# A Strassen stage turned into a graph with one fixed order per engine, and two more weight sets multiplied by seven products in the second layer

## The chip, the core and the metric

The kernel runs on one core of a Trainium2 chip. The metric is the device time of one execution in microseconds; before the change the median of three runs is 882.67 us (882.40 to 883.54). The engines are TensorE (PE in the profile; PEld are its weight loads), VectorE (DVE), ScalarE (ACT), GpSimd (POOL) and SyncE (SP), whose queue issues the DMAs here.

## What is computed

Causal attention with a decay for 4 x 8 heads of 576 tokens and 64 columns, and on its output, 2304 tokens of 512 columns, a mixture of four experts that all see every token:

```python
x = attention(q, k, v, f)                       # 2304 x 512
p = probs / (probs.sum(-1, keepdims=True) + 1e-09)
out = np.zeros((2304, 512))
for e in range(4):
    h = np.maximum(x @ w1[e], 0.0)              # 512 -> 1024
    out += p[:, e:e + 1] * (h @ w2[e])          # 1024 -> 512
```

The 4 x 1024 hidden columns are cut into 16 pairs p of 2 x 128 columns; a pair holds the rows of w1 and w2 that belong to them.

## The kernel before, in words

Every matmul of the expert layers is made of three in float16 (high x high, high x low, low x high halves), which keeps float32 accuracy. Attention and the experts of the first five chunks of 256 tokens come first and fill TensorE until about 566 us. The last four chunks (5 to 8, 1024 tokens) are done by the Strassen stage behind it, and the change is in this stage alone.

**First layer of a pair** (`Big`, L1339 on). The 512 columns of x and the 256 hidden columns of the pair are blocks of a 2 x 2 Strassen-Winograd product with seven products instead of eight. A product (`product`, L1346) is six matmuls of 128x512 into a PSUM bank. Seven steps `l1(s)` per pair follow each product by copies to SBUF (ScalarE, L1381), sums with what is there (VectorE, `plus`, L1386), relu (ScalarE, L1390) and the splitting into a high and a low half of h (`halves`: ScalarE L1369, VectorE L1370). For pairs whose second layer is also done by seven products, four more sums s 1 to s 4 of blocks of h are made on GpSimd (`sum`, L1395), each with its own halves.

**Second layer of a set** (`Second`, L1457 on). The sets are (0), (1), (2, 3), (4, 5) up to (14, 15). A set in `PLAIN` = (0, 1, 6, 7, 12, 13) takes 16 parts, each six matmuls of 128x512 for two pairs; every second one is followed by a gather of 128x512 into the accumulator (`gather`, VectorE, L1129). Any other set takes seven products: 28 parts of six matmuls of 128x256, each followed by a gather of 128x256. A bank is reused by the next product on it only after that gather has read it. Parts are dealt out between the first-layer steps of the pairs two places ahead, in a queue that is spread evenly (`give`); the set (14, 15) ends the kernel alone.

**Weights.** `split_1(p)` loads the float32 block of w1 (`raw_half`, L1237, 512 KB) and its ready float16 halves, makes four sums of blocks (GpSimd, L1232, tile wt), scales them (ScalarE, L1259), and splits them (ScalarE L1263, GpSimd L1264, tile bs). `split_2(p)` does the same for w2 where the set is not plain (tiles wu, bt; ScalarE L1304, VectorE L1308); for a plain pair it only loads the halves (tile bv).

**What sets the order.** TensorE's matmuls of the stage are chained one by one in program order (`in_line`). The other engines' instructions are placed by the framework's scheduler, which simulates a timeline, with a few hand-written bounds: weight steps come after the latest copy and gather (`in_turn`), the weight sums after the latest GpSimd sum (`pool`). The weight work of a pair is staged by hand over three places of the first-layer steps (`staged`).

Of the kernel before, what the change touches and what calls it, by code (L numbers as in the profile page):

```python
# [13 lines left out]
ALU = mybir.AluOpType  # L14
# [32 lines left out]
AHEAD_W = 6  # L47
JOBS = ((0, 0), (1, 0), (2, 0), (3, 0), (0, 1), (1, 1), (2, 1), (3, 1))
# [32 lines left out]
EXPONENT = 0x7F800000  # L81


@with_exitstack
def fused(ctx: ExitStack, tc: tile.TileContext, qk, v, f, probs, w, out):
# [907 lines left out]
    def w_pair(n):  # L993
        t = w_p.tile([128, 2, 1024], F16, tag="w", name=f"w{n}")
        wh[n], wl[n] = t[:, 0], t[:, 1]
        return t
# [117 lines left out]
    def gather(c, tt, sc, ps, times, d0=0, d1=DM):  # L1114
# [8 lines left out]
        if begun == {False}:  # L1123
            nc.vector.tensor_scalar(
                out=acc[c][:, tt, d0:d1], in0=ps, scalar1=sc, scalar2=None, op0=ALU.mult
            )
        else:
            gone.append(
                nc.vector.scalar_tensor_tensor(  # L1129
                    out=acc[c][:, tt, d0:d1],  # L1130
                    in0=ps,
                    scalar=sc,
                    in1=acc[c][:, tt, d0:d1],
                    op0=ALU.mult,
                    op1=ALU.add,
                )
            )
        done = [d for (_, _, d) in keys if seen[c, tt, d] == times[d // 256]]
        if done:
            a, z = done[0], done[-1] + 256  # L1140
            for o, r0, n in rows_of(c, tt):
                nc.sync.dma_start(out=out[r0 : r0 + n, a:z], in_=acc[c][o : o + n, tt, a:z])

# [43 lines left out]
    PLAIN = (0, 1, 6, 7, 12, 13)  # L1187
# [16 lines left out]
    def x_piece(i, k, op=None, *of):  # L1204
# [10 lines left out]
        if op is None:  # L1215
            x = x_of(k)
        else:
            x = xs_[k, i] = late.x.tile([128, 2, CH], F32, tag="wx", name=f"rx{k}_{i}", bufs=2)
            pool.append(nc.gpsimd.tensor_tensor(out=x, in0=x_of(of[0]), in1=x_of(of[1]), op=op))
# [3 lines left out]
    def sums(name, r, table):  # L1223
        part = lambda b: r[:, b[0], 256 * b[1] : 256 * b[1] + 256]
        if not hasattr(late, "x"):
            t = acc_p.tile([128, 4, 256], F32, tag="acc", name=name)
        else:
            t = late.x.tile([128, 4, 256], F32, tag="wt", name=name, bufs=2)
        w_of = lambda b: part(b) if type(b) is tuple else t[:, b - 1, :]
        for k, a, z, op in table:  # L1230
            with tc.issue_after(pool[-1].ins) if pool else nullcontext():
                nc.gpsimd.tensor_tensor(out=t[:, k - 1, :], in0=w_of(a), in1=w_of(z), op=op)  # L1232
        return t.rearrange("p k n -> p (k n)")

    def raw_half(p, k):
        r = wr_p.tile([128, 2, 512], F32, tag="wr", name=f"wr{NS + p}_{k}", bufs=4)
        nc.sync.dma_start(  # L1237
            out=r,
            in_=w[2 * p : 2 * p + 2, :, 512 * k : 512 * k + 512].rearrange("n p c -> p n c"),
        )  # L1240
        return r

    def split_1(p):
        if p >= 16:
            return ()
        r = raw_half(p, 0)
        t, u = (
            w_p.tile([128, 2, 1024], F16, tag="w", name=f"b{k}{p}") for k in ("w", "s")
        )
        one = t.rearrange("p n (s f) -> p n s f", s=2)  # L1250
        for n in range(2):
            nc.sync.dma_start(out=one[:, n], in_=wd[2 * p + n][:, :, :512])
        bw[p] = one, u.rearrange("p s (k f) -> p s k f", k=4)
        f = sums(f"wt{p}", r, SUMS)
        hi, lo = u[:, 0], u[:, 1]

        def scale(a):
            x = f[:, a : a + 512]
            nc.scalar.activation(out=x, in_=x, func=AF.Copy, scale=wsc[:, p // 2, 0:1])  # L1259

        def part(a):
            x, h = f[:, a : a + 512], hi[:, a : a + 512]
            nc.scalar.activation(out=h, in_=x, func=AF.Copy)  # L1263
            nc.gpsimd.tensor_tensor(out=lo[:, a : a + 512], in0=x, in1=h, op=ALU.subtract)  # L1264

        return (
            lambda: scale(0),
            lambda: (part(0), scale(512)),
            lambda: part(512),
        )  # L1270

    seconds = []

    def second_tile(name):
        i = len(seconds) % 8
        if i < 4:
            t = wr_p.tile([128, 2, 1024], F16, tag="wk", name=name, bufs=4)
        elif i < 6:
            t = w_p.tile([128, 2, 1024], F16, tag="w", name=name)
        else:  # L1280
            t = late.x.tile([128, 2, 1024], F16, tag="wx", name=name, bufs=2)
        seconds.append(t)
        return t

    def split_2(p):
        if p >= 16:
            return ()
        t = second_tile(f"bv{p}")
        one = t.rearrange("p n (s f) -> p n s f", s=2)
        for n in range(2):  # L1290
            nc.sync.dma_start(out=one[:, n], in_=wd[2 * p + n][:, :, 512:])
        if p in PLAIN:
            bv[p] = one, None
            return ()
        r = raw_half(p, 1)
        u = second_tile(f"bt{p}")
        bv[p] = one, u.rearrange("p s (k f) -> p s k f", k=4)
        f = sums(f"wu{p}", r, TSUMS)
        hi, lo = u[:, 0], u[:, 1]
        sc = wsc[:, p // 2, 1:2]  # L1300

        def upper(a):
            z = a + 512
            nc.scalar.activation(out=hi[:, a:z], in_=f[:, a:z], func=AF.Copy, scale=sc)  # L1304

        def lower(a):
            z = a + 512
            nc.vector.scalar_tensor_tensor(  # L1308
                out=lo[:, a:z],
                in0=f[:, a:z],  # L1310
                scalar=sc,
                in1=hi[:, a:z],
# [4 lines left out]
        return (  # L1317
            lambda: upper(0),
            lambda: (lower(0), upper(512)),
            lambda: lower(512),  # L1320
        )
# [7 lines left out]
    line, mark, pool, gone = [], [], [], []  # L1329
# [9 lines left out]
    class Big:  # L1339


        def __init__(self, p):
            self.p = p
            self.h, self.ps = {}, {}

        def product(self, m, bank, start):  # L1346
            if start:
                self.ps[bank] = ps_a.tile([128, 512], F32, tag="a", name=f"m{self.p}_{m}")
            ps = self.ps[bank]
            w_, b = PRODUCTS[m]  # L1350
            a, z = part_of(bw[self.p], w_)
            for k in range(2):
                o = slice(128 * k, 128 * k + 128)
                for i, (lhsT, rhs) in enumerate(((a, rh[b]), (a, rl[b]), (z, rh[b]))):
                    in_line(
                        out=ps,
                        lhsT=lhsT[:, o],
                        rhs=rhs[:, k, :],
                        start=(start and k == 0 and i == 0),
                        stop=(k == 1 and i == 2),  # L1360
                        skip_group_check=True,
                    )
            return ps

        def halves(self, b, x, op=ALU.mult, tag=None):

            t = late.h.tile([128, 2, 512], F16, tag=f"h{tag or b}", name=f"h{self.p}_{b}")
# [466 lines left out]
```

## Time and profile before

| | |
|---|---|
| median of three runs | 882.67 us (882.40 to 883.54) |
| profiled execution, its own time | 883.93 us |
| its span, first to last instruction | 882.1 us |
| TensorE busy | 864.4 us, 98% |
| VectorE busy | 643.0 us, 73% |
| ScalarE busy | 480.6 us, 54% |
| GpSimd busy | 372.6 us, 42% |

Busy time is the union of an engine's instructions, and neighbours overlap a little, so a mean duration is somewhat more than an instruction's place in its queue. An idle time is put down to what ended it (the releaser). The engine shares are means over stages; for this change the busy table of single stretches says more.

### The profile page before, as it was taken

Reading aid. Unit: us, or ns where it says so; the run is one execution under the profiler, and the core shown is the slowest. Engines: PE = TensorE matmul, PEld = TensorE weight load, DVE = VectorE, ACT = ScalarE, POOL = GpSimd, SP = SyncE. Lnnn points to the kernel's source line nnn. Section 1 sums busy time; section 2 is a strip of 40 time slices with the busy share of each in tenths; the row PEclk is TensorE's granted clock in tenths of the full one; section 3 lists DMA queues with packets and bytes.
Section 4 is the critical chain, followed back from the end, with each engine's and each line's share of the span. In section 5 each row is a group of like instructions: output and inputs, shape, how many; then the busy total and the mean of one; then the engine's idle time right before and its main releaser. Section 6 shows DMA issues by size and latency. Waiting matters only on the chain.

```text
span 882.1 us, 16028 instructions
## 1 busy us (share of the span) xinstructions
PE 864.4 (98%) x5699; PEld 556.8 (63%) x5699; DVE 643.0 (73%) x1390; ACT 480.6 (54%) x999; POOL 372.6 (42%) x421
## 2 busy tenths in 40 slices
PE   9999999999999999999999999999989999999998
PEld 5766666666766766667666766544456654666547
DVE  5766799868777888767678856456788657886586
ACT  5473645746565866555577644356555355554350
POOL 4253423542322432243232203827787437884160
PEclk9999999999999999999999999999999999999999
DMA  9989697799999999958979951533124332240003
GB/s 276 391 212 361 135 298 232 194 327 247 250 249 246 271 280 251 265 137 217 295 196 282 258 89 42 189 122 120 48 81 135 121 120 71 72 145 25 25 1 96
DMA packets 166589, 162.49 MB, mean 184 GB/s; under 512 B 104854, under 2 KB 129484, under 8 KB 166508
## 3 DMA queue, kind: packets, MB, share of 16 engines
q1 hardware_dynamic: 166508, 161.46, 65.9%
q8 instruction: 45, 0.74, 0.4%
q14 instruction: 36, 0.29, 0.1%
HBM read 115.65 MB, written 21.64 MB: 156 GB/s over the span
## 4 chain that ended last, share of the span: by engine, by line
PE 65%; POOL 10%; DVE 9%; DMA 6%; ACT 5%; issue 4%; SPq 1%; POOLq 0%; DVEq 0%; ACTq 0%
PE l L1100 18%; PE l L1057 16%; PE y L1335 8%; PE m L1335 8%; PE s L666 4%; POOL s L1395 4%; PE o L870 4%; PE l L1045 3%; POOL wt L1232 3%; PE s L689 2%; DMA raw<-in_qk 2%; POOL wu L1232 2%; DMA pt<-z 1%; DVE acc L1129 1%; ACT wt L1259 1%
## 5 line engine op out<-in xcount | busy, mean ns | idle before, releaser
L1057 PE MATMUL l<-y,w 128*128 128x256 f16 x1728 | 211.5, 273 | 0.0
L1057 PEld LDWEIGHTS <-w 128*128 128x128 f16 x1728 | 163.9, 98 | 40.1 <-issue 7.4
L1100 PE MATMUL l<-w,gh 128*128 128x512 f16 (+1 forms) x600 | 184.4, 392 | 2.8 <-DVE acc L1129 2.8
L600 POOL CAST q<-raw 64x320 fp32r<-64x320 f32 (+1 forms) x56 | 25.2, 452 | 224.9 <-PE s L689 101.5
L1100 PE MATMUL l<-w,gl 128*128 128x512 f16 x284 | 107.2, 379 | 0.3 <-DVE gl L1074 0.3
L716 ACT ACTIVATE p<-p,nm 128x384 f32<-128x384 f32 (+3 forms) x96 | 62.0, 646 | 64.6 <-DVE nm L701 64.5
L1129 DVE SCALAR_TENSOR_TENSOR acc<-y,scg,acc 128x256 f32<-128x256 f32 (+1 forms) x164 | 81.2, 515 | 14.9 <-PE y L1335 14.7
L1335 PE MATMUL m<-rh,bs 128*128 128x512 f16 x256 | 86.4, 379 | 0.0
L1100 PEld LDWEIGHTS <-gh 128*128 128x128 f16 x568 | 51.1, 98 | 51.9 <-issue 10.9
L607 POOL TENSOR_TENSOR kl<-raw,hi 64x576 fp32r<-64x576 f32 (+1 forms) x56 | 66.5, 1187 | 38.3 <-ACT hi L598 36.8
L701 DVE CUSTOM_DVE_ANT_0 p<-s,mask 128x384 f32<-128x384 f32 (+3 forms) x96 | 54.3, 572 | 28.2 <-PE s L666 25.4
L804 DVE SCALAR_TENSOR_TENSOR z<-p,rs,z 128x512 f16<-128x512 f32 x96 | 61.0, 677 | 18.9 <-ACT z L803 18.9
L1264 POOL TENSOR_TENSOR bs<-wt,bs 128x512 f16<-128x512 f32 x32 | 37.9, 1190 | 78.8 <-ACT bs L1263 77.8
L1074 DVE SCALAR_TENSOR_TENSOR gl<-l,gh 128x512 f16<-128x512 f32 x72 | 49.1, 682 | 24.0 <-ACT gh L1069 23.4
L598 ACT ACTIVATE hi<-raw 128x896 fp32r<-128x896 f32 (+1 forms) x56 | 45.0, 808 | 38.5 <-DMA raw<-in_qk 18.1
L1335 PE MATMUL m<-rh,bw 128*128 128x512 f16 x191 | 64.4, 379 | 1.0 <-ACT r L1381 0.8
L803 ACT ACTIVATE z<-p,rs 128x512 f16<-128x512 f32 x96 | 52.9, 613 | 22.5 <-issue 8.0
L1335 PEld LDWEIGHTS <-bs 128*128 128x128 f16 x384 | 37.6, 98 | 38.5
L1370 DVE SCALAR_TENSOR_TENSOR h<-s,h 128x512 f16<-128x512 f32 x40 | 46.3, 1164 | 17.8 <-ACT h L1369 17.5
L1069 ACT ACTIVATE gh<-l 128x512 f16<-128x512 f32 (+1 forms) x80 | 46.9, 586 | 22.3 <-PE l L1057 19.5
L1381 ACT ACTIVATE r<-m 128x512 f32<-128x512 f32 x58 | 33.9, 587 | 41.5 <-PE m L1335 34.1
L1335 PEld LDWEIGHTS <-h 128*128 128x128 f16 x480 | 46.9, 98 | 14.8 <-issue 2.6
(401 smaller groups left out, 1754.2 us busy)
## 6 DMA issues: line engine op xcount, KB each, us to landing
wr<-in_w SPq DMA_DIRECT2D x64, 512.0 KB
wd<-w SPq DMA_DIRECT2D x32, 512.0 KB
w<-wd SPq DMA_DIRECT2D x32, 512.0 KB
raw<-in_qk SPq DMA_DIRECT2D x32, 448.0 KB
wp<-in_w SPq DMA_DIRECT2D x36, 256.0 KB
bv<-wd SPq DMA_DIRECT2D x32, 256.0 KB
bw<-wd SPq DMA_DIRECT2D x32, 256.0 KB
raw<-in_qk SPq DMA_DIRECT2D x24, 256.0 KB
```

What stands on the lines that cost most here:

```text
L607: nc.gpsimd.tensor_tensor(out=kl[:64, :wk], in0=r[:64, ko : ko + wk], in1=hi[:64, ko : ko + wk].bitcast(F32), op=ALU.subtract,)
L701: nc.vector.tensor_tensor_reduce(out=pt[:, a:z], in0=ps, in1=mask2 if t == 4 and n else mask[:, m0 + a : m0 + z], scale=-0.125, scalar=BIG ...
L716: nc.scalar.activation(out=pt[:, :w_], in_=pt[:, :w_], func=AF.Exp, scale=-1.0, bias=self.nmax[hh][:, c : c + 1], accum_out=self.ssum[:, h ...
L803: nc.scalar.activation(out=o[:, 0], in_=x, func=AF.Copy, scale=sc)
L804: nc.vector.scalar_tensor_tensor(out=o[:, 1], in0=x, scalar=sc, in1=o[:, 0], op0=ALU.mult, op1=ALU.subtract)
L1057: nc.tensor.matmul(out=self.l1p[:, fi, :], lhsT=lhsT, rhs=rhs[:, k, :], start=(k == 0 and m == 0), stop=(k == 3 and m == 2),)
L1069: self.first = nc.scalar.activation(out=self.gh, in_=self.l1p, func=AF.Relu)
L1074: self.last = nc.vector.scalar_tensor_tensor(out=self.gl, in0=self.l1p, scalar=0.0, in1=self.gh, op0=ALU.max, op1=ALU.subtract,)
L1100: matmul(out=l2[tt], lhsT=lhsT, rhs=rhs, start=(opens and fi == 0 and m == 0), stop=(closes and fi == 1 and m == len(parts) - 1),)
L1129: nc.vector.scalar_tensor_tensor(out=acc[c][:, tt, d0:d1], in0=ps, scalar=sc, in1=acc[c][:, tt, d0:d1], op0=ALU.mult, op1=ALU.add,)
L1335: line.append(nc.tensor.matmul(**args))
L1370: nc.vector.scalar_tensor_tensor(out=t[:, 1], in0=x, scalar=0.0 if relu else 1.0, in1=t[:, 0], op0=op, op1=ALU.subtract,)
```

## The change

1. `PLAIN` becomes (0, 1): sets (6, 7) and (12, 13) take seven products too, so 14 of the 16 pairs do (10 before).
2. Sum s 1 of a pair is no longer a ScalarE relu copy from PSUM and a GpSimd sum, but one VectorE instruction that reads PSUM (`sum_1`).
3. From pair 1 on, every step of the stage is not issued at once but recorded as an `Op` with its engine, an estimated cost (in units of about 0.22 us) and the tiles that it reads, writes and opens. `Flow.go` then works out for each the latest end that keeps TensorE's fixed order without a wait, and plays the engines forward: on each engine, of the operations that could start within 0.2 units of the first, the one with the least such end goes next. A VectorE operation that shares memory with a running GpSimd one is taken as up to 1.7 times as long. The order so found is chained instruction by instruction on ScalarE, VectorE and GpSimd (`emit`); SP's loads are recorded but not chained.
4. The hand-written bounds (`in_turn`, `pool`, `staged`) go; in the part ahead of pair 1, which is still issued directly, GpSimd's weight sums are no longer held behind its sums of x.

The diff, cut to its core:

```diff
+LAG = {"PE": 1.5, "DVE": 0.5, "ACT": 0.5, "POOL": 0.5, "SP": 24}
+class Flow:
+    def add(self, engine, cost, run, reads=(), writes=(), new=(), shared=False):
...
+        if engine == "PE":
+            o.deps.add(self.pe)
+            self.pe = o
...
+        if self.direct:
+            o.end = -99.0
+            self.emit(o)
+        else:
+            self.ops.append(o)
+    def go(self):
...
+        for o in self.ops:
+            if o.engine == "PE":
+                o.late = t
+                t += o.cost
...
+        for o in reversed(line):
+            o.late = min(o.late, t)
+            for d in o.deps:
+                d.late = min(d.late, o.late - lag(d, o) - d.cost)
...
+            for c in best.values():
+                t = min(r for r, _ in c) + 0.2
+                picks.append((t, min((x for x in c if x[0] <= t), key=lambda x: x[1].late)))
+            _, (t, o) = min(picks, key=lambda x: x[0])
+            cost = o.cost
+            if o.shared and free["POOL"] > t:
+                cost = min(1.7 * cost, max(cost, free["POOL"] - t + 0.4 * cost))
+            o.end = free[o.engine] = t + cost
+            left.remove(o)
+            self.emit(o)
...
-    PLAIN = (0, 1, 6, 7, 12, 13)
+    PLAIN = (0, 1)
...
+    def emit(o):
+        chain = chains.get(o.engine) if not flow.direct else None
+        with tc.issue_after(chain.ins) if chain else nullcontext():
+            i = o.run()
+        if i is not None:
+            chains[o.engine] = i
...
-            with tc.issue_after(pool[-1].ins) if pool else nullcontext():
-                nc.gpsimd.tensor_tensor(out=t[:, k - 1, :], in0=w_of(a), in1=w_of(z), op=op)
+            flow.add(
+                "POOL",
+                3.8,
+                lambda k=k, a=a, z=z, op=op: one(k, a, z, op),
...
-                    self.copy(ps, r[1, 0], AF.Relu)
-                    self.sum(1, r[0, 0], r[1, 0], ALU.add)
-                    self.halves(1, self.s[1])
+                    self.sum_1("a")
+                    self.halves(1, ("s", 1), ALU.mult)
...
+                return nc.vector.scalar_tensor_tensor(
+                    out=self.s[1],
+                    in0=self.ps[bank],
+                    scalar=0.0,
+                    in1=self.r[0, 0],
+                    op0=ALU.max,
+                    op1=ALU.add,
+                )
...
-    def in_turn(f_):
-        with tc.issue_after(mark[-1].ins), tc.issue_after(gone[-1].ins):
-            f_()
-
-    staged(1, 0, split_1, 2)
...
+    flow.direct = False
+    todo = {(1, 0): [(split_1, 2)], (1, 1): [(split_2, 2)], (1, 3): [(split_1, 3)], (1, 4): [(split_2, 3)]}
     for p in range(4, 16):
-        staged(p - 2, 0, split_1, p)
-        staged(*((p, 2) if p % 2 == 0 else (p - 1, 5)), split_2, p)
+        todo.setdefault((p - 2, 0), []).append((split_1, p))
+        todo.setdefault((p, 2) if p % 2 == 0 else (p - 1, 5), []).append((split_2, p))
...
     for f_ in queue + Second(SETS[-1]).parts():
         f_()
+    flow.go()
     late.close()
```

## Rows read from the trace of the kernel before

**Rows 1.** The page: busy us, share of the span and instructions of each engine.

```profile
PE 864.4 (98%) x5699; PEld 556.8 (63%) x5699; DVE 643.0 (73%) x1390; ACT 480.6 (54%) x999; POOL 372.6 (42%) x421
```

**Rows 2.** Busy table: stretch, length, PE, PEld, DVE, ACT, POOL, granted clock, DMA share, GB/s.

```profile
632.00:670.00 38.00, 34.36 (x230) 22.43 (x231) 31.37 (x50) 22.05 (x39) 30.02 (x28) 1.00 0.26 85
670.00:708.00 38.00, 36.58 (x252) 24.41 (x251) 27.04 (x49) 15.26 (x26) 21.82 (x23) 1.00 0.37 124
747.00:785.00 38.00, 37.58 (x253) 24.54 (x252) 31.76 (x50) 22.50 (x40) 29.80 (x28) 1.00 0.31 98
785.00:822.00 37.00, 35.59 (x248) 23.92 (x246) 26.44 (x48) 15.03 (x26) 18.89 (x19) 1.00 0.14 44
822.00:860.00 38.00, 38.00 (x187) 17.98 (x185) 25.15 (x32) 18.15 (x31) 15.94 (x12) 1.00 0.05 15
760.00:780.00 20.00, 19.58 (x135) 13.00 (x134) 18.48 (x28) 12.26 (x22) 15.78 (x14) 1.00 0.26 80
```

**Rows 3.** Waits of TensorE from 540 us on: total us, times, longest.

```profile
PE y L1335 <- DVE acc L1129: 6.6, 12, 1.4
PE l L1100 <- DVE acc L1129: 1.6, 2, 1.3
PE m L1335 <- ACT r L1381: 0.8, 2, 0.4
PE y L1335 <- DVE h_(0, 1)_7885 L1370: 0.4, 1, 0.4
```

**Rows 4.** VectorE in order of time: start, us, what, [idle before <- releaser].

```profile
647.61 1.56 DVE L1308 SCALAR_TENSOR_TENSOR bt<-wu,wsc,bt 128x512 f16<-128x512 f32 x1
649.09 1.75 DVE L1370 SCALAR_TENSOR_TENSOR h<-s,h 128x512 f16<-128x512 f32 x1
...
651.37 1.16 DVE L1370 SCALAR_TENSOR_TENSOR h_(0, 1)_8087<-r,h_(0, 1)_8087 128x512 f16<-128x512 f32 x1
652.45 0.47 DVE L1129 SCALAR_TENSOR_TENSOR acc<-y,scg,acc 128x256 f32<-128x256 f32 x1
...
678.72 1.23 DVE L1370 SCALAR_TENSOR_TENSOR h<-s,h 128x512 f16<-128x512 f32 x1 [2.01 <-ACT h L1369]
679.87 0.47 DVE L1129 SCALAR_TENSOR_TENSOR acc<-y,scg,acc 128x256 f32<-128x256 f32 x1
```

**Rows 5.** The chain that ended last: start, us, engine, tile, line, count.

```profile
596.84 1.29 PE y L1335 x6
...
599.43 1.29 PE y L1335 x6
...
682.50 1.31 PE y L1335 x12
```

**Rows 6.** VectorE's costliest groups from 566 us on: count, busy us, mean ns, idle before.

```profile
L1129 DVE SCALAR_TENSOR_TENSOR acc<-y,scg,acc 128x256 f32<-128x256 f32 x140 | 63.5, 477 | 14.9 <-PE y L1335 14.7
L1370 DVE SCALAR_TENSOR_TENSOR h<-s,h 128x512 f16<-128x512 f32 x40 | 46.3, 1164 | 17.8 <-ACT h L1369 17.5
L1386 DVE TENSOR_TENSOR r<-m,r 128x512 f32<-128x512 f32 x47 | 32.0, 682 | 16.7 <-ACT r L1381 13.5 <-PE m L1335 3.1
L1308 DVE SCALAR_TENSOR_TENSOR bt<-wu,wsc,bt 128x512 f16<-128x512 f32 x20 | 20.6, 1040 | 4.1 <-ACT bt L1304 4.1
```

**Rows 7.** GpSimd's groups from 566 us on, in the same form.

```profile
L1264 POOL TENSOR_TENSOR bs<-wt,bs 128x512 f16<-128x512 f32 x30 | 35.7, 1192 | 76.3 <-ACT bs L1263 75.3 <-DMA wr<-in_w 0.8
...
L1395 POOL TENSOR_TENSOR s<-r,r 128x512 f32<-128x512 f32 x15 | 21.4, 1424 | 37.7 <-ACT r L1381 37.7
```

**Rows 8.** All engines in order of time, around the start of the last set.

```profile
856.18 1.75 DVE L1370 SCALAR_TENSOR_TENSOR h_(0, 1)_10135<-r,h_(0, 1)_10135 128x512 f16<-128x512 f32 x1
...
859.56 0.49 PE L1335 MATMUL y<-bv,h_(0, 1)_10012 128*128 128x256 f16 x3
...
860.14 0.74 DVE L1129 SCALAR_TENSOR_TENSOR acc<-y,scg,acc 128x512 f32<-128x512 f32 x1
860.80 0.68 DVE L1370 SCALAR_TENSOR_TENSOR h<-s,h 128x512 f16<-128x512 f32 x1
```

More of the change, by code (lines that the diff above doesn't have):

```diff
@@ L1274, in second_tile @@
     def second_tile(name):
         i = len(seconds) % 8
+        seconds.append(name)
         if i < 4:
[L1277 to L1283, printed above, removed]
-    def split_2(p):
[L1286 to L1291, printed above, removed]
-        if p in PLAIN:
[L1293 to L1299, printed above, removed]
+            return flow.slot("wk", 4), lambda: wr_p.tile(
+                [128, 2, 1024], F16, tag="wk", name=name, bufs=4
+            )
@@ L1315, in lower @@
             )
[L1317 to L1321, printed above, removed]
+        for i in range(2):
+            f_ = [(base, 2 * i + 1), (base, 2 * i + 2)]
+            flow.add(
+                "ACT",
+                2.5,
+                lambda a=512 * i: upper(a),
+                reads=f_,
+                writes=[(u_, ("h", i))],
+                new=[u_] if i == 0 else [],
+            )
+            flow.add(
+                "DVE",
+                3.3,
+                lambda a=512 * i: lower(a),
+                reads=f_ + [(u_, ("h", i))],
+                writes=[(u_, i)],
+                shared=True,
+            )
     def part_of(pair, b):
@@ L1350, in product @@
             w_, b = PRODUCTS[m]
[L1351 to L1362, printed above, removed]
@@ L1380, in copy, with run @@
-        def copy(self, ps, x, func=AF.Copy):
-            mark.append(nc.scalar.activation(out=x, in_=ps, func=func))
-        def plus(self, ps, b):
-            x = self.r[b]
-            nc.vector.tensor_tensor(out=x, in0=ps, in1=x, op=ALU.add)
+            def run():
+                if start:
+                    self.ps[bank] = ps_a.tile([128, 512], F32, tag="a", name=f"m{self.p}_{m}")
+                a, z = part_of(bw[self.p], w_)
+                for k in range(2):
+                    o = slice(128 * k, 128 * k + 128)
+                    for i, (lhsT, rhs) in enumerate(((a, rh[b]), (a, rl[b]), (z, rh[b]))):
+                        in_line(
+                            out=self.ps[bank],
+                            lhsT=lhsT[:, o],
+                            rhs=rhs[:, k, :],
+                            start=(start and k == 0 and i == 0),
+                            stop=(k == 1 and i == 2),
+                            skip_group_check=True,
+                        )
@@ new lines, in copy, with run, plus, relu @@
+        def copy(self, bank, b, func=AF.Copy, new=False):
+            def run():
+                if new:
+                    self.open()
+                return nc.scalar.activation(out=self.r[b], in_=self.ps[bank], func=func)
+            flow.add(
+                "ACT",
+                2.5,
+                run,
+                reads=[(self.bank[bank], 0)],
+                writes=[self.rk[b]],
+                new=self.r_new if new else [],
+            )
+        def plus(self, bank, b):
+            def run():
+                x = self.r[b]
+                return nc.vector.tensor_tensor(out=x, in0=self.ps[bank], in1=x, op=ALU.add)
+            def relu():
+                x = self.r[b]
+                return nc.scalar.activation(out=x, in_=x, func=AF.Relu)
+            k = self.rk[b]
+            flow.add("DVE", 2.8, run, reads=[(self.bank[bank], 0), k], writes=[k])
@@ L1397, in open @@
         def open(self):
             p = self.p
-            self.seven = p not in PLAIN
             if p % 2:
```

519 lines of the change are left out of this document (372 added, 147 removed).

## The prediction, made before the changed kernel was run

> **What bounds the kernel now.** I read the page's engine shares and clock first: TensorE is busy 98% of the span, no other engine over 73% [rows 1], and the granted clock is full (1.00, the 2.4 GHz level) in every stretch read here [rows 2]. So time can go in two ways only: fewer columns through TensorE, or fewer gaps in it. Then the busy table by stretches, cut where one second-layer set ends and the next begins [rows 2]. The Strassen stage is the last 320 us or so. In two of its stretches the first layer of two pairs with seven second-layer products runs beside the second layer of such a pair set (632 to 670, 747 to 785), and there VectorE is busy 31.4 and 31.8 us of 38; where one side is plain it has 25 to 27. TensorE's missing time sits in the first of them (3.6 us of 38) and in the two stretches behind them (1.4 each), little in the second (0.4) and none from 822 to 860. The list of waits says on what: 6.6 us in 12 waits for a gather into acc, 0.8 for a copy out of PSUM, 0.4 for a half of h; 7.8 us in the stage, without its end [rows 3].
>
> Why a gather of 0.47 us is late, VectorE's order in time shows [rows 4]. TensorE's longest wait, 1.4 us, ends with the gather that starts at 652.45, and this stood behind a bt lower half of 1.56 us (weights needed a set later), an h<-s of 1.75 and an h_(0, 1) of 1.16. At 678.72 it is the other fault: the queue stands 2.01 us with nothing running, blocked by an h<-s whose upper half waits for a GpSimd sum, and a gather for which TensorE waits starts behind it at 679.87. Both are orders, not lack of capacity.
>
> **Part 1, seven products for sets (6, 7) and (12, 13).** A plain set has 16 parts of 6 matmuls of 512 columns; a seven set 28 parts of 6 with 256. The chain of waits, where it runs along TensorE, gives both prices: a part and a product of six 512s each take 2.59 us from 596.84 to 599.43, so 1.295 each; twelve of 256 take 1.31 [rows 5]. Plain: 16 x 1.295 = 20.7 us. Seven: 14 x 1.31 = 18.3 us. Two sets: -4.8 us of pure TensorE time, on the path, since TensorE runs without a gap in the stretch 822 to 860, which is one of the two. That is the one term without doubt.
>
> What it adds elsewhere, per pair: four wu sums on GpSimd, two bt halves each on ScalarE and VectorE, the relu copies and four more h, and per set 28 gathers of 256 in place of 8 of 512; on the SP queue one more 512 KB load of weights, four in all [rows 6, 7]. All of it must hide under TensorE. A stretch of two seven pairs is 14 x (1.295 + 1.31) = 36.5 us of TensorE work. VectorE's share: successive instructions overlap by 0.08 us (the bt of 1.56 from 647.61 is followed at 649.09 [rows 4]), so I take 0.08 off each mean of [rows 6]: 28 gathers 11.1, 8 h<-s 8.7, 4 bt 3.8, 6 r<-m,r 3.6, two h_(0, 1) between 1.16 and 1.75 say 2.7, four undisturbed h of 0.68 [rows 8] 2.4. With part 2 below, 33.5 us, or 92% of 36.5. (The two dense stretches as they are, 31.4 and 31.8 with 1.2 of part 2 on top, say 33.0 at the most, which agrees.) GpSimd: 30.0 in a dense stretch [rows 2], less two sums of 1.42 that part 2 takes: 27.2, 75%. ScalarE: 22.5 less two copies, some 60%. So TensorE stays the longest, but VectorE has 8% to spare where it had a third in the plain stretches, and there are now six such stretches in a row (second layers of sets (2, 3) to (12, 13) beside first layers of pairs 4 to 15) where there were two. That it can run so densely is seen in its busiest 20 us, 18.5 of 20, 92% [rows 2]. Loads cost GpSimd 0.8 us of waiting in the whole stage [rows 7]; if each of the four more cost as much, 3.2 us in all, GpSimd's slack of 9 us a stretch covers it. Without that cover it would come out as a gap of the same size.
>
> **Part 2, the first sum on VectorE.** s 1 = relu(PSUM) + r goes to VectorE straight from the bank; a ScalarE copy and a GpSimd sum (1.42) per pair go. No row has this operation; the nearest are r<-m,r (one PSUM and one SBUF input, 128x512) at 0.68 [rows 6], which I take, so 0.60 in the queue, 1.2 us per stretch, beside TensorE. Its bounds are an undisturbed queue place of 0.60 and a blocked one of 1.67, as for the h, 2.1 us more per stretch, all of it still within 36.5. It could also be a gain: GpSimd stood 37.7 us in nine waits for that copy [rows 7], with sums behind it that h halves and so VectorE waited for.
>
> What it spares in the shared memory port is small: GpSimd's work per stretch falls from 30.0 to 27.2. An h<-s lasts 0.68 free and up to 1.75 [rows 4, 8]. The Trainium skill (SBUF — State Buffer, Who interferes with whom) says that a VectorE instruction with two SBUF inputs and a reading GpSimd instruction exclude each other, the later one blocking until the first is done. The trace agrees in direction (that spread), and its mean of 1.16 [rows 6] says that most are blocked in part only. What full blocking would make of the time is the third rival.
>
> **Part 3, the order.** Gaps of 7.8 us in the stage go if the order puts each gather ahead of what can wait. TensorE's own order does not change. I do not take all of it: a fixed order is made with fixed prices, while an h takes 0.68 to 1.75, and there are six dense stretches. The nearest row is the second dense stretch, whose own gap is 0.4 of 38 with the same work less 1.2 us of VectorE; I take 0.6 per dense stretch, bounds 0 and 1.8 (its 0.4 with the 1.4 of the stretch behind it [rows 2]). 6 x 0.6 = 3.6. The end: seven parts of 0.655 us, 4.6 us, now stand between the last first-layer product and the last set, where six plain parts of 1.295, 7.8 us, stood; the last set needs its h_(0, 1) first, which was done at 857.9, 1.7 us before the set began at 859.56, and then a gather that began at 860.14 behind an h [rows 8]. A cover that is 3.2 us shorter, against 1.7 to spare, costs at most 1.5, less what the order puts ahead. I take 1.0 there and 0.4 at the stage's start: 5.0 in all, against 7.8: -2.8 us. Bounds: 0 (-7.8) and 12.2 (+4.4). The last gather and store stay as they are.
>
> The stretch before the stage also loses an order: the early sums no longer wait behind the x sums. Its waits on TensorE are 1.6 us, two [rows 3], so it is worth from -1.6 to about +1.6; I take 0, since nothing says which way.
>
> **The sum.** Against the profiled execution, 883.9 us of which 882.1 are span: -4.8 - 2.8 = -7.6, so 876.3. The median of the runs is 882.67; the same difference gives 875.1. About 0.2% (1.8 us) is what a measurement of this kernel can tell from no change.
>
> **Rivals.**
> 1. The order gives nothing beyond what density takes: each dense stretch loses 1.8, as the second one does with its spill, plus the same 1.4: gaps of 12.2 in place of 7.8, +4.4, against -4.8: 882.3, no change. For it: the second dense stretch is the work as planned well already. Against: its spill is a blocked queue, which an order by slack mends.
> 2. VectorE sets the pace (slower). In the two dense stretches it reached 83 and 84% of the time [rows 2]. If in-order waits hold it at 84%, 33.5 us take 39.9, 3.4 over TensorE's 36.5, six times: gaps 20.4 + 1.4 = 21.8 in place of 7.8, +14.0 - 4.8: 891.9. It decides from 87% downwards (38.3 per stretch). For it: every half of h hangs on a chain from TensorE over VectorE, ScalarE and GpSimd to VectorE again. Against: the 20 us at 92%, and that its idle time then was partly that TensorE gave it nothing to do.
> 3. Full blocking at the port: 14 instructions per stretch with two SBUF inputs (8 h<-s, 4 bt, 2 h_(0, 1)) at 1.67 in place of their 15.2 in sum make 23.4, VectorE 41.7, 5.2 over, six times: about 903. The means of 1.16 and 1.04 speak against it.
> 4. Better: all gaps go and the stretch before the stage gains as well: below 870.
>
> **How the numbers follow.** Forecast 0.70 (own range 870 to 880.5), rival 1 0.13, rival 2 0.11, rival 3 0.02, rival 4 0.04. Faster: 0.74; same: 0.13; slower: 0.13. The range takes in the forecast and rival 1 and leaves out rivals 2 and 3 and the far end of 4: 869.5 to 884.
>
> **What would show it.** Right: TensorE's busy time some 4.8 us less; in stretches cut at the sets, 36.5 to 37.5 us each and VectorE at 89 to 92%; waits of y for acc down to 3 or 4 us; no VectorE queue standing on an h<-s with a gather behind it. Rival 2 shows as gaps of 2 to 3 us in every stretch with VectorE at 84 to 87% and its idle put down to ScalarE's h; rival 3 as a mean h<-s over 1.5. Wrong altogether would be GpSimd late on its loads (waits of s or wt for DMA), or a gap of over 2 us ahead of the last set.

## The result, and the profile after

The changed kernel takes 874.11 us (four runs, 873.64 to 874.35), 0.9898 of the kernel before, with a 95% interval of 0.9881 to 0.9915. A second measurement, in a later job, gave 873.89 us and 0.9871 (0.9848 to 0.9894). The prediction was 875.1 us in a range of 869.5 to 884. The profiled execution took 873.64 us, of which 871.8 are span; before it was 883.93 and 882.1, so 10.3 us less.

The page's busy times of the changed kernel, to be set beside [rows 1]:

```profile
PE 858.9 (99%) x5843; PEld 570.9 (65%) x5843; DVE 675.9 (78%) x1464; ACT 494.6 (57%) x1021; POOL 392.6 (45%) x439
```

TensorE has 5.5 us less to be busy with, although it runs 144 matmuls more (shorter ones), and VectorE has 33 us more. The busy table, cut where the sets (2, 3), (4, 5) and so on begin (columns as in [rows 2]):

```profile
631.60:670.40 38.80, 37.02 (x253) 24.59 (x252) 34.56 (x56) 21.06 (x36) 23.85 (x23) 1.00 0.27 88
670.40:706.90 36.50, 36.50 (x254) 24.68 (x253) 33.42 (x54) 23.35 (x41) 29.65 (x29) 1.00 0.36 111
706.90:745.40 38.50, 37.32 (x253) 24.58 (x252) 32.68 (x54) 21.37 (x37) 31.56 (x30) 1.00 0.40 130
745.40:782.40 37.00, 36.72 (x254) 24.69 (x253) 34.13 (x58) 24.76 (x43) 25.96 (x27) 1.00 0.35 113
782.40:818.90 36.50, 36.50 (x254) 24.63 (x253) 32.36 (x54) 19.34 (x33) 30.32 (x28) 1.00 0.21 68
818.90:850.20 31.30, 31.30 (x230) 22.32 (x229) 29.49 (x53) 16.78 (x29) 8.89 (x7) 1.00 0.00 1
```

Two of the dense stretches last 36.5 us and show TensorE without a gap, VectorE at 92 and 89%; in [rows 2] the dense ones had it at 83 and 84%. The others are less even: the first and the third last 38.8 and 38.5 us, and in the third VectorE has only 85%. The sixth is short because it holds 230 matmuls and not some 253: part of its first layer has run before. The waits of TensorE from 540 us on, beside [rows 3]:

```profile
PE y L1527 <- DVE acc L1223: 2.0, 4, 0.6
PE m L1527 <- ACT r L1614: 1.1, 3, 0.6
PE l L1195 <- DVE acc L1223: 1.1, 1, 1.1
PE l L1195 <- ACT gh L1164: 0.7, 1, 0.7
PE l L1195 <- DVE gl L1169: 0.5, 1, 0.5
```

The stage itself loses 3.1 us in this list (7.8 before), the stretch ahead of it 2.3 (1.6 before).

**A gap is more than its idle time.** How much the stage lost is better read from start to start. Here is TensorE in order of time in the changed kernel (start, us, what, [idle before <- releaser]):

```profile
632.24 0.49 PE L1527 MATMUL y<-bv,h_(0, 1)_7755 128*128 128x256 f16 x3
632.56 0.49 PE L1527 MATMUL y<-bv,h_(0, 1)_7924 128*128 128x256 f16 x3
633.63 0.38 PE L1527 MATMUL m<-rh,bs 128*128 128x512 f16 x1 [0.57 <-ACT r L1614]
```

Three matmuls of 256 follow each other in 0.33 us, so the m could have started at 632.89; it starts 0.74 later, and the row says 0.57, because the last matmul's own end lies behind the next one's possible start. In all the sums below, gaps are counted that way: each start against the pace of 0.216 us per 512 columns and 0.109 per 256, above 0.06 us, in the one profiled execution of each kernel. The stage before lost 10.9 us so counted, the changed one 4.9. From the first part of the second layer to the last group of matmuls it was 294.2 us and is 283.5 (867.21 less 583.67): 10.7 less, of which 6.0 are gaps and 4.7 work.

### The profile page after: what moved, and what is told of

Its sections match the earlier page's. It is cut to its first block, busy times and chain, and to the rows that moved or that the text cites. A ratio compares the mean times of both kernels' runs of the same rounds, so it can differ in the third digit from the quotient of the medians.

```text
span 871.8 us, 16423 instructions
## 1 busy us (share of the span) xinstructions
PE 858.9 (99%) x5843; PEld 570.9 (65%) x5843; DVE 675.9 (78%) x1464; ACT 494.6 (57%) x1021; POOL 392.6 (45%) x439
## 4 chain that ended last, share of the span: by engine, by line
PE 67%; DVE 12%; POOL 8%; DMA 5%; ACT 4%; issue 3%; SPq 1%; ACTq 0%; POOLq 0%; DVEq 0%
PE l L1195 18%; PE l L1152 15%; PE y L1527 10%; PE m L1527 8%; PE s L760 4%; PE o L964 3%; PE l L1140 3%; POOL wt L1344 3%; DMA raw<-in_qk 3%; DVE acc L1223 2%; PE s L783 2%; POOL bs L1416 2%; DVE w L1108 2%; DMA pt<-z 1%; DVE h L1590 1%
## 5 line engine op out<-in xcount | busy, mean ns | idle before, releaser
L1223 DVE SCALAR_TENSOR_TENSOR acc<-y,scg,acc 128x256 f32<-128x256 f32 (+1 forms) x204 | 93.8, 484 | 4.7 <-PE y L1527 4.6
L1195 PEld LDWEIGHTS <-gh 128*128 128x128 f16 x568 | 51.1, 98 | 51.3 <-issue 10.7
L1527 PEld LDWEIGHTS <-h 128*128 128x128 f16 x672 | 65.7, 98 | 18.0 <-issue 0.6
L1527 PE MATMUL y<-bt,h 128*128 128x256 f16 x504 | 61.1, 273 | 0.3 <-DVE acc L1223 0.3
L1590 DVE SCALAR_TENSOR_TENSOR h<-s,h 128x512 f16<-128x512 f32 x56 | 58.2, 1050 | 2.0 <-ACT h L1584 1.7
L1416 POOL TENSOR_TENSOR bs<-wt,bs 128x512 f16<-128x512 f32 x32 | 42.5, 1338 | 35.9 <-ACT bs L1410 35.9
L1164 ACT ACTIVATE gh<-l 128x512 f16<-128x512 f32 (+1 forms) x80 | 46.9, 586 | 20.6 <-PE l L1152 17.8
```

The costliest lines, as they stand in the source:

```text
L1195: matmul(out=l2[tt], lhsT=lhsT, rhs=rhs, start=(opens and fi == 0 and m == 0), stop=(closes and fi == 1 and m == len(parts) - 1),)
L1223: i = nc.vector.scalar_tensor_tensor(out=acc[c][:, tt, d0:d1], in0=ps, scalar=sc, in1=acc[c][:, tt, d0:d1], op0=ALU.mult, op1=ALU.add,)
L1416: return nc.gpsimd.tensor_tensor(out=u[:, 1, a : a + 512], in0=got["f"][:, a : a + 512], in1=u[:, 0, a : a + 512], op=ALU.subtract,)
L1527: line.append(nc.tensor.matmul(**args))
L1590: return nc.vector.scalar_tensor_tensor(out=t[:, 1], in0=at_[key], scalar=0.0 if relu else 1.0, in1=t[:, 0], op0=op, op1=ALU.subtract,)
```

## The experiments

All times are medians; ratios are against the kernel before, run on the same chip beside it, since that one moved between 883.1 and 884.5 from job to job. "Gaps" are those of the stage from the first part of its second layer on, counted as above.

| run | us | ratio (95%) | gaps, us |
|---|---|---|---|
| before | 883.1 to 884.5 | 1 | 10.9 |
| changed | 874.11 | 0.9898 (0.9881 to 0.9915) | 4.9 |
| changed, again | 873.89 | 0.9871 (0.9848 to 0.9894) | 4.9 |
| order alone | 876.03 | 0.9910 (0.9897 to 0.9923) | 2.3 |
| seven products alone | 889.05 | 1.0057 (1.0041 to 1.0073) | 19.8 |
| s 1 on GpSimd again | 872.71 | 0.9872 (0.9859 to 0.9885) | 4.5 |
| program order for slack | 877.55 | 0.9930 (0.9917 to 0.9943) | 8.9 |
| planned, not chained | 874.22 | 0.9894 (0.9880 to 0.9907) | 5.6 |
| 3 more on VectorE per pair | 870.34 | 0.9841 (0.9819 to 0.9863) | 2.6 |
| 9 more on VectorE per pair | 877.72 | 0.9939 (0.9926 to 0.9951) | 9.0 |
| seven products everywhere | 880.27 | 0.9963 (0.9951 to 0.9976) | 12.0 |
| early GpSimd chain | 872.32 | 0.9857 (0.9833 to 0.9881) | 4.9 |
| dearer blocking | 873.29 | 0.9872 (0.9851 to 0.9893) | 4.1 |
| early chain and margin | 867.32 | 0.9822 (0.9808 to 0.9835) | 0.6 |

### The order alone, the seven products alone

The changed kernel with the old set of plain pairs:

```diff
-    PLAIN = (0, 1)
+    PLAIN = (0, 1, 6, 7, 12, 13)
```

> The new order and the sum s 1 on VectorE, but sets (6, 7) and (12, 13) plain as before. Theory (the two parts add: 4.8 us of TensorE work from the seven products, the rest from the order): TensorE's work stays as before and its gaps in the stage fall from 7.8 to 2 or 3 us, so about 4 us under the kernel before, 878.5 to 879.5. Rival (the order only makes room for the denser VectorE work and gives nothing where that is not dense): no change, 882.5 to 883.5.

Measured: 876.03 us, 8.4 under the kernel before on the same chip. The direction is the theory's, the size is twice as large as expected: gaps fell from 10.9 to 2.3 where I had reckoned with 7.8 to 2 or 3. So the order alone gives most of the change's gain. "The order" is here all of it together: the plan by slack, its chain, and the end of the hand-written bounds.

The kernel before with the new set of plain pairs (the same two lines, the other way round):

> The kernel before with seven products in sets (6, 7) and (12, 13) and nothing else: old order, old sum s 1. Theory (in the old order each dense stretch loses 1.8 to 5 us): 4.8 us less work, gaps of 12 to 25 in place of 7.8, so 882 to 895, most likely near 887, slower than before. Rival (the seven products give their 4.8 us whatever the order): 878.

Measured: 889.05 us, slower than before by 0.57%, where the theory stood. Busy table and TensorE's main wait of that kernel:

```profile
672.00:711.00 39.00, 36.85 (x251) 24.28 (x250) 32.53 (x53) 22.59 (x40) 30.98 (x29) 1.00 0.35 112
711.00:750.00 39.00, 36.87 (x253) 24.48 (x252) 32.54 (x52) 22.61 (x41) 30.99 (x29) 1.00 0.32 105
750.00:789.00 39.00, 36.88 (x252) 24.48 (x251) 32.54 (x52) 22.77 (x40) 30.98 (x29) 1.00 0.33 109
```

```profile
PE y L1335 <- DVE acc L1129: 13.5, 24, 1.4
```

Stretch for stretch the same picture: VectorE at 32.5 of 39.0, 83%, and TensorE waiting for gathers, some 2.8 us a stretch counted from start to start. This is the picture of the second rival of the prediction, come true without the new order: 4.7 us of work saved, 8.9 us of gaps more. With the new order the same step is worth about 2 us (876.0 to 873.9 or 874.1, from different jobs, and the intervals of 0.9910 and 0.9898 overlap): the saved 4.7 less the gaps that went from 2.3 to 4.9. So the two parts don't add; the second needs the first.

### The first sum

The sum s 1 as a ScalarE copy and a GpSimd sum again, planned in the graph:

```diff
-                    self.sum_1("a")
+                    self.copy("a", (1, 0), AF.Relu)
+                    self.sum(1, (0, 0), (1, 0), ALU.add, new=True)
... (and `sum` opens the tiles of the sums, as `sum_1` did)
```

> The changed kernel with the sum s 1 as before: a ScalarE relu copy and a GpSimd sum per pair, planned in the graph. VectorE has 1.2 us per stretch less to do, GpSimd 2.8 more. Theory (GpSimd and ScalarE have room, and VectorE is not yet the bound): within 1.5 us of the changed kernel, 873 to 875.5. Rival (the chain of GpSimd sums is what is late, and s 1 on it delays every later half of h): 1 us per dense stretch, 879 to 881.

Measured: 872.71 us, 0.9872, beside 0.9871 and 0.9898 for the changed kernel, and gaps of 4.5 beside 4.9. Moving this sum is worth nothing that could be told; the theory stands, the rival falls.

### What in the order does it

Among the operations that could start, the one that stands first in the program instead of the one with the least slack:

```diff
-                picks.append((t, min((x for x in c if x[0] <= t), key=lambda x: x[1].late)))
+                picks.append((t, min((x for x in c if x[0] <= t), key=lambda x: x[1].n)))
```

> The changed kernel, but of the operations that could start, the one that stands first in the program goes next, not the one with the least slack. Graph, costs and fixed order stay. Theory (the gain of the order is that gathers go ahead of weight halves and h that can wait): gaps come back, 1 to 3 us per dense stretch, 879 to 892. Rival (any order made with good costs does; slack is a detail): within 1.5 us of the changed kernel, 873 to 875.5.

Measured: 877.55 us, gaps 8.9. The gaps come back as the theory had it, but fewer: 4.0 us in all, 0.7 per dense stretch where it had 1 to 3, and the time lies just under its range of 879 to 892. The rival's 873 to 875.5 is missed as well. The longest gap, 2.43 us on TensorE at 693.68, has the old look in VectorE's order (compare [rows 4]):

```profile
687.19 1.01 DVE L1482 SCALAR_TENSOR_TENSOR bt<-wu,wsc,bt 128x512 f16<-128x512 f32 x1
688.45 1.44 DVE L1482 SCALAR_TENSOR_TENSOR bt<-wu,wsc,bt 128x512 f16<-128x512 f32 x1 [0.24 <-ACT bt L1476]
690.04 3.19 DVE L1590 SCALAR_TENSOR_TENSOR h<-s,h 128x512 f16<-128x512 f32 x2
693.15 0.47 DVE L1223 SCALAR_TENSOR_TENSOR acc<-y,scg,acc 128x256 f32<-128x256 f32 x1
```

Two weight halves and two h stand ahead of the gather. But beside the old order with the same products (the seven products alone, gaps of 19.8) even this plan takes 10.9 us of the gaps away, and slack the next 4.0.

The plan is issued in its order, but no instruction is chained to the one before it:

```diff
-        chain = chains.get(o.engine) if not flow.direct else None
+        chain = None
```

> The changed kernel, planned as it is and issued in the planned order, but without chaining an instruction to the one before it on ScalarE, VectorE and GpSimd, so that the framework's scheduler may move them by its own simulated timeline. Theory (the fixed order is what removes the gaps, and the scheduler would let weight halves and h go ahead of gathers again): gaps of 8 to 20 us, 877 to 889. Rival (the order in which the program issues them is enough): within 1.5 us of 874.

Measured: 874.22 us, gaps 5.6. Here my theory of the time fell: the chain adds nothing that can be told. But it was not the planned order that ran. From 540 us on, 243 of the 429 pairs of neighbours on VectorE are others than in the changed kernel, as many as in the run by program order (241). The scheduler did move the operations, and marks of the old order are back (VectorE's two groups, then the busy table, cut where the sets (2, 3) to (8, 9) begin):

```profile
L1590 DVE SCALAR_TENSOR_TENSOR h<-s,h 128x512 f16<-128x512 f32 x56 | 48.6, 869 | 16.0 <-ACT h L1584 15.9
L1482 DVE SCALAR_TENSOR_TENSOR bt<-wu,wsc,bt 128x512 f16<-128x512 f32 x27 | 28.4, 1068 | 1.7 <-ACT bt L1476 1.6
```

```profile
630.90:667.40 36.50, 36.50 (x254) 24.64 (x253) 30.75 (x55) 22.51 (x40) 26.87 (x25) 1.00 0.30 93
667.40:705.20 37.80, 36.84 (x253) 24.63 (x252) 30.93 (x55) 21.69 (x38) 28.54 (x26) 1.00 0.36 112
705.20:743.30 38.10, 37.17 (x253) 24.59 (x252) 31.13 (x56) 22.92 (x40) 29.58 (x28) 1.00 0.36 111
743.30:781.40 38.10, 36.87 (x253) 24.65 (x252) 31.23 (x55) 22.00 (x38) 28.84 (x26) 1.00 0.35 110
```

VectorE's queue stands 16.0 us on an h<-s (17.8 in [rows 6], 2.0 in the changed kernel), and yet TensorE loses hardly more. The same instructions keep VectorE busy for 31 us a stretch here and for 32.4 to 34.6 in the changed kernel, since an h<-s lasts 869 ns for 1050. So the planned order itself is not what removes the gaps: a rather different one, without the hand-written bounds and issued from the plan, does about as well. Which of these two does it is not shown: a kernel without the bounds, issued in program order without a plan, was not run.

### How much room VectorE has

Three, then nine instructions more per pair, each reading 256 columns of PSUM into a scratch tile:

```diff
... (`probe`: one `tensor_scalar` from the bank into the scratch tile)
             flow.add("DVE", 2.8, run, reads=[(self.bank[bank], 0), k], writes=[k])
+            for _ in range(1 if self.p > 1 else 0):     # 3 in the second run
+                flow.add("DVE", 1.8, probe, reads=[(self.bank[bank], 0)], writes=[("probe", 0)])
```

> The changed kernel with three more VectorE instructions for each pair from 2 on, known to the planner: each reads 256 columns of a PSUM bank behind a plus and writes a scratch tile nobody reads, 0.39 us of the queue, 2.3 us per dense stretch. VectorE then has 35.8 of 36.5 us. Theory (VectorE has some 3 us per stretch to spare and hides them, at the price of a few more gaps): 1 to 6 us over the changed kernel, 875 to 880. Rival 1 (VectorE is the bound already, every added us shows): 14 us or more, 888 and up. Rival 2 (hidden without loss): within 1 us.

Measured: 870.34 us, faster than the changed kernel by some 3.5 us, with more work. All three expectations missed. The two intervals overlap, but in the stage itself gaps fell from 4.9 to 2.6; the rest of the 3.5 lies ahead of it, where the two programs are the same. Its dense stretches:

```profile
670.40:706.90 36.50, 36.05 (x250) 24.29 (x249) 34.13 (x60) 24.61 (x43) 30.97 (x30) 1.00 0.38 127
706.90:743.40 36.50, 36.50 (x254) 24.66 (x252) 33.50 (x60) 20.93 (x36) 28.30 (x29) 1.00 0.32 105
743.40:780.00 36.60, 36.60 (x254) 24.74 (x253) 34.35 (x63) 23.02 (x40) 27.19 (x26) 1.00 0.39 130
780.00:816.50 36.50, 36.50 (x253) 24.57 (x252) 34.81 (x58) 19.11 (x33) 29.35 (x29) 1.00 0.18 59
```

VectorE has 92 to 95%, and TensorE hardly waits. So the gaps left in the changed kernel are not VectorE's load; they belong to that plan. Another plan, here one that had to place more, has fewer.

> The changed kernel with nine more VectorE instructions for each pair from 2 on (as the run with three, which took 870.3 us with 94% of VectorE in the dense stretches): 7.0 us more per dense stretch than the changed kernel, 39 to 40 of work against TensorE's 36.5. Theory (TensorE is the bound up to 36.5 us of VectorE per stretch, VectorE beyond it): about 3 us over in each of six stretches and 3 or 4 in the last, 886 to 898. Rival (each added us shows from the start): 42 us more, 915. Rival (VectorE has more room than counted): under 880.

Measured: 877.72 us, well under the theory's 886, and the rival with more room was right. The stretches (cut at even times):

```profile
670.00:708.00 38.00, 37.43 (x259) 25.11 (x257) 37.32 (x73) 22.00 (x39) 25.82 (x25) 1.00 0.33 107
708.00:746.00 38.00, 37.84 (x260) 25.20 (x258) 37.25 (x76) 21.04 (x36) 23.92 (x22) 1.00 0.29 94
746.00:784.00 38.00, 38.00 (x266) 25.85 (x265) 37.56 (x73) 22.96 (x39) 27.75 (x27) 1.00 0.39 125
784.00:822.00 38.00, 37.30 (x256) 24.85 (x255) 37.40 (x73) 22.50 (x38) 28.13 (x28) 1.00 0.30 98
822.00:857.00 35.00, 31.44 (x228) 22.15 (x227) 34.65 (x69) 18.69 (x31) 19.80 (x19) 1.00 0.01 1
```

VectorE is busy 98 to 99%, and TensorE still loses only about 2.5 of the 9.0 us before 822; the rest of the gaps lie behind, where work that was put off has to be done. Of the 7.0 us more per stretch some 3 fill the room that VectorE had, part moves to other stretches (39.2 us of VectorE for 33.9 ahead of the dense ones, 20.0 for 15.0 in the last set), and some 2 are made up by shorter instructions. VectorE's groups with two SBUF inputs, first of this kernel, then of the changed one (count | busy us, mean ns | idle before):

```profile
L1590 DVE SCALAR_TENSOR_TENSOR h<-s,h 128x512 f16<-128x512 f32 x56 | 52.8, 949 | 0.6 <-ACT h L1584 0.5
L1482 DVE SCALAR_TENSOR_TENSOR bt<-wu,wsc,bt 128x512 f16<-128x512 f32 x28 | 22.5, 817 | 0.0
```

```profile
L1590 DVE SCALAR_TENSOR_TENSOR h<-s,h 128x512 f16<-128x512 f32 x56 | 58.2, 1050 | 2.0 <-ACT h L1584 1.7
L1482 DVE SCALAR_TENSOR_TENSOR bt<-wu,wsc,bt 128x512 f16<-128x512 f32 x28 | 24.4, 873 | 3.2 <-ACT bt L1476 3.1
```

The two h_(0, 1) per stretch fell most, from 1449 to 968 ns in the mean. In [rows 6] the two groups had 1164 and 1040, so VectorE's work per stretch is not the fixed number that my sum made of it. Nor does it simply fall as VectorE fills: with three more instructions h<-s has 987 but bt 954, and unchained, with none more, 869 and 1068.

### Seven products everywhere

```diff
-    PLAIN = (0, 1)
+    PLAIN = ()
...
-        i = len(seconds) % 8
+        i = (len(seconds) + 6) % 8
```

> The changed kernel with seven products in the single sets (0) and (1) as well (and the second-layer weight tiles dealt out from another slot, so that they fit). TensorE has 2.4 us less to do. But in the two stretches of a single set the gathers do not halve: 28 gathers (11.1 us) and the first layer of one pair (11.2) make 22.3 us of VectorE against 18.2 of TensorE. Theory (VectorE sets the pace there): 2 to 8 us over the changed kernel, 876 to 882. Rival (TensorE's work decides here too): 871 to 872.

Measured: 880.27 us, 6 us over the changed kernel, within the theory's range. The busy table where the single sets run:

```profile
580.00:600.00 20.00, 18.92 (x104) 9.89 (x102) 18.14 (x26) 14.37 (x26) 11.59 (x10) 1.00 0.22 69
600.00:620.00 20.00, 18.60 (x122) 11.71 (x121) 19.95 (x41) 12.01 (x21) 15.98 (x16) 1.00 0.41 132
620.00:640.00 20.00, 19.22 (x130) 12.49 (x129) 19.62 (x35) 11.24 (x19) 13.55 (x12) 1.00 0.26 80
```

From 600 on VectorE is full and TensorE is not: up to the start of set (2, 3) TensorE has gaps of 3.5 us, where the changed kernel has none, and these eat up the 2.4 that were saved. A seven set costs VectorE 28 gathers whether it sums over one pair or two; so here the saving of TensorE's columns pays for a set of two and not for a set of one. The change leaves just these two sets plain. But that is the smaller part of the 6 us. Behind the single sets the gaps grew from 4.9 to 8.5, and the last 234 matmuls ahead of the second layer take 44.0 us for 42.9. Whether work that was put off, another plan or the moved weight tiles cause those is not shown.

### The stretch ahead, the planner's prices, and a faster version

GpSimd's operations chained in the directly issued part too:

```diff
-        chain = chains.get(o.engine) if not flow.direct else None
+        chain = chains.get(o.engine) if not flow.direct or o.engine == "POOL" else None
```

> The changed kernel with GpSimd's operations of the directly issued part (the weight sums of pairs 0 and 1) chained in program order as well, which holds them behind the sums of x as before. Theory (the loose order there is what moved the gaps just before the stage from 1.6 to 2.2 us): 0.3 to 0.6 us under the changed kernel, hardly to be told in the time; in the trace the gaps between 540 and 568 us go back to about 1.6. Rival (those gaps have nothing to do with it): they stay at 2.2.

Measured: 872.32 us beside 873.89 on the same chip. TensorE's waits ahead of the stage fell from 2.3 us to one:

```profile
PE l L1195 <- DVE acc L1223: 1.0, 1, 1.0
```

The direction is the theory's, and the gain is larger than expected, about 1.6 us, though the two intervals overlap. The last 234 matmuls ahead of the second layer say the same: 42.2 us in the kernel before, 42.9 in the changed one, 41.4 here. So the chain gives back what the change had lost there and as much again.

A VectorE operation that meets a running GpSimd one may count as up to 2.5 times as long in the plan:

```diff
-                cost = min(1.7 * cost, max(cost, free["POOL"] - t + 0.4 * cost))
+                cost = min(2.5 * cost, max(cost, free["POOL"] - t + 0.4 * cost))
```

> The changed kernel, but the planner may take a VectorE operation that meets a running GpSimd one as up to 2.5 times as long, not 1.7 (in the trace such an h lasts 1.75 us and 0.68 free). Theory (the gaps left come from operations that last longer than the plan has them): gaps fall from 4.9 to about 3, 1 to 2 us under the changed kernel. Rival (the gaps left are a matter of VectorE's density, not of prices): within 1 us of it either way.

Measured: 873.29 us, gaps 4.1: within what the rival said, a little towards the theory. The first gaps of the stage went and others came. This price alone decides nothing.

> The changed kernel unaltered, beside the next three on one chip. Its three 5 us against the kernel before with seven products alone and 2 us against the order alone came from different chips; here it is expected at 0.990 of the kernel before, as at first.

It measured 873.89 us, 0.9871, and its gaps are those of the first execution, each within a few hundredths of a microsecond: the gaps belong to the program, not to the execution.

Early chain, and every VectorE operation planned 10% longer than the change has it:

```diff
         self.engine, self.cost, self.run, self.shared = engine, cost, run, shared
+        if engine == "DVE":
+            self.cost = 1.1 * cost
... (and the line of the early chain, as above)
```

> The early chain on GpSimd (872.3 us on its own) and a plan in which every VectorE operation counts as 10% longer than before. Theory (a plan with margin on its fullest engine leaves fewer gaps): the gaps of 4.9 us fall to 2 or 3, 869.5 to 871. Rival (which gaps remain is chance of the plan, not margin): gaps between 2 and 6, 870 to 874.

Measured: 867.32 us, 0.9822 (0.9808 to 0.9835), the fastest of all: 0.3 to 0.4% under the early chain alone, 4.3 us fewer gaps, and below both expectations. In the waits of TensorE from 540 us on the stage is left with 0.2 us:

```profile
PE l L1197 <- DVE acc L1225: 1.0, 1, 1.0
PE y L1529 <- DVE acc L1225: 0.2, 1, 0.2
```

One of the gaps that went, in VectorE's order at the first dense stretch, changed kernel first, then this one:

```profile
632.35 1.73 DVE L1590 SCALAR_TENSOR_TENSOR h<-s,h 128x512 f16<-128x512 f32 x1
634.00 1.64 DVE L1482 SCALAR_TENSOR_TENSOR bt<-wu,wsc,bt 128x512 f16<-128x512 f32 x1
635.57 0.74 DVE L1223 SCALAR_TENSOR_TENSOR acc<-y,scg,acc 128x512 f32<-128x512 f32 x1
```

```profile
629.50 1.15 DVE L1592 SCALAR_TENSOR_TENSOR h<-s,h 128x512 f16<-128x512 f32 x1
630.58 0.74 DVE L1225 SCALAR_TENSOR_TENSOR acc<-y,scg,acc 128x512 f32<-128x512 f32 x1
631.24 1.09 DVE L1484 SCALAR_TENSOR_TENSOR bt<-wu,wsc,bt 128x512 f16<-128x512 f32 x1
632.25 0.47 DVE L1225 SCALAR_TENSOR_TENSOR acc<-y,scg,acc 128x256 f32<-128x256 f32 x1
```

In the changed kernel two operations that may be blocked stand in a row and last 3.2 us, and TensorE waits 0.62 at 636.36 for the gather behind them; in the other plan a gather stands between. That margin in the prices, and not just another throw of the plan, removes the gaps rests on two plans that reckon with more on VectorE than the changed kernel's does (this one and the one with three more instructions), against one with a single dearer price; that is an indication, not a proof.

## Why the prediction was right, and where it was off

- **TensorE's work, -4.8 us.** Measured 4.7, from the start-to-start lengths less their gaps. On the path, as argued from [rows 2] and [rows 5].
- **The order, -2.8 us.** Right in kind, less than half of what came: -6.0. Two things were mis-sized. The first is the 7.8 us of gaps in [rows 3]: the list counts idle time after a matmul's modelled end, and leaves out about 0.16 us per gap and the gaps that are shorter than that; from start to start it was 10.9. The second is what would be left. The 5.0 was made from busy tables and waits, so it is to be set beside the list's 3.1 and not beside 4.9: in the list's own count the order gave -4.7. The 3.6 for the six dense stretches fits that 3.1 in sum and not in kind, which is luck: almost all of it lies in the stretches of sets (2, 3) and (6, 7), and the stretches of (4, 5), (10, 11) and (12, 13) have next to none.
- **Why the order helps.** The prediction has it that each gather goes ahead of what can wait. The waits for gathers did fall, from 6.6 to 2.0 us, and VectorE's standing on an h<-s from 17.8 to 2.0. But the unchained run has 16.0 of the latter and about the same gaps, so a standing queue does not by itself make TensorE wait. That the plan's order does it, and not the end of the hand-written bounds, is argued and not shown.
- **The end, 1.0 us.** It cost nothing: behind 747.2 us the changed kernel has one gap of 0.07. The cover was also miscounted: it is nine parts and not seven, 844.28 to 850.17, 5.9 us for 4.6, and the h_(0, 1) that the last set needs was done at 849.55.
- **The start of the stage, 0 between -1.6 and +1.6.** It cost 0.7: over the last 234 matmuls ahead of the second layer 42.9 us for 42.2 (its first part starts at 583.67 for 583.08), and the early chain run gives back more than that. "Nothing says which way" was too easy: an order was taken away and nothing put in its place.
- **VectorE 33.5 us per dense stretch.** Measured 32.4 to 34.6, and TensorE stays the longest. The sum is met in part by luck: h<-s took 1050 ns for 1164 and bt 873 for 1040, which makes 1.6 us less per stretch by my sum, and the queue was overlapped less than I took it to be. The unchained run does the same work in 31 in four of its stretches.
- **The sum.** 876.3 was forecast for the profiled execution, 873.64 came: work -4.7 for -4.8, gaps -6.0 for -2.8, the start +0.6 for 0, and -0.2 between the last matmul and the end. The medians differ by 9.0 us where 7.6 were forecast.
- **Rival 1** (the order gives nothing) falls with the run of the order alone. **Rival 2** (VectorE held at 84%) is what the old order does to the seven products: 83% and 889 us. With the new order five of the six stretches have 89 to 94%, and the runs with more work on VectorE 92 to 99. The third, 706.90 to 745.40, shows the rival's own sign: 85%, 2.1 us of gaps, and VectorE's idle mostly put down to ScalarE. **Rival 3** (full blocking at the port) goes the other way: the mean of h<-s fell from 1164 to 1050 ns. On GpSimd's side the bs lower halves rose from 1192 to 1328 ns; with seven products alone they had 1176, with the order alone 1334. So in these four kernels bs went with the order and not with the load, and bt did too, the other way: 1040 and 1067 in the old order, 873 and 908 in the new. What the Trainium skill (SBUF — State Buffer, Who interferes with whom) says of the later one blocking fits that in direction. It is no rule for a sum: with nine more instructions on VectorE both are short (bs 1247, bt 817). The bs of the changed kernel, of the order alone and of the seven products alone:

```profile
L1416 POOL TENSOR_TENSOR bs<-wt,bs 128x512 f16<-128x512 f32 x28 | 36.9, 1328 | 35.9 <-ACT bs L1410 35.9
L1416 POOL TENSOR_TENSOR bs<-wt,bs 128x512 f16<-128x512 f32 x28 | 37.0, 1334 | 39.8 <-ACT bs L1410 39.8
L1264 POOL TENSOR_TENSOR bs<-wt,bs 128x512 f16<-128x512 f32 x29 | 34.1, 1176 | 50.5 <-ACT bs L1263 49.8 <-DMA wr<-in_w 0.6
```

Part 2 was costed at 1.2 us of VectorE per stretch, hidden; the run without it could not tell it from nothing, and s<-m,r took 0.69 us for the 0.68 that was taken from r<-m,r.

What stays open: whether the plan or the end of the hand-written bounds gives the order its gain, why exactly the margin's plan leaves almost no gaps, and whether the same margin would do so for another set of stages.

## What to carry to other kernels

Removing work from the bound engine is worth what the next engine's order allows: here the same saving cost 4.6 us with one order of VectorE and gave about 2 with another, so look to the order of the helpers first. When a plan is laid on fixed prices and some instructions last one to two and a half times as long as when free, try a margin on the fullest engine (here it took the gaps from 4.9 to 0.6 us, in one plan), and look in the trace for pairs of such instructions ahead of one that the bound engine needs. Chaining the planned order was not needed; run it unchained before you credit the exact order. Count gaps from start to start against the pace, not by the idle time shown.

## What the runs showed of the hardware that I had not expected

How long the same VectorE instruction lasts in the mean depends on what it is run beside, and more than I had thought. An h<-s of 128x512, 0.68 us when free, took 1164 ns before, 1132 with seven products alone, 1117 with the order alone, 1050 in the changed kernel, 987 and 949 with three and nine more instructions, and 869 unchained; a bt lower half 1040, 1067, 908, 873, 954, 817 and 1068. Neither the order nor VectorE's load alone explains all of these. I had taken the means of [rows 6] as fixed, and so put the point at which VectorE would set the pace too early: 7.0 us more per stretch, 40.5 against 36.5 by my sum, cost 4 to 6 us in the whole kernel (0.9939 beside 0.9898 and 0.9871).
